# The last segment's output products begin with the linear branch's rows instead of the attention's, and the instruction list is laid out anew

## The chip, the cores and the metric

The kernel runs on one core of one Trainium2 chip. The metric is the device time of one execution in microseconds (us), as the median of several runs. Less is better.

## The reference

Two attention branches read the same input x (2048 rows of 640 columns, bfloat16), and a gate per row mixes their results. Names that begin with A belong to the linear branch, names with B to the memory branch.

```python
# g = sigmoid(sum(x * gate_w));  out = g * A + (1 - g) * B;  32 heads of 20 columns
# A, the linear branch
q, k, v = split(x @ wqkv)
phi(t)  = concat(softmax(t @ w_phi), softmax(-(t @ w_phi)))
A = (phi(q) @ (phi(k).T @ v)) / (phi(q) @ sum(phi(k)) + 1e-6) @ A_wo
# B, the memory branch: 4 segments of 512 rows, one after the other
for s in range(4):
    a_dot = softmax(q_s @ k_s.T * scale + causal mask) @ v_s
    a_mem = (pq @ M) / (pq @ z + 1e-6)        # pq = elu(q_s) + 1
    o_s   = g_h * a_mem + (1 - g_h) * a_dot   # g_h = sigmoid(beta), per head
    M, z  = M + pk.T @ v_s, z + sum(pk)       # pk = elu(k_s) + 1
B = concat(o) @ B_wo
```

Each branch ends in its own product with a 640 x 640 matrix. The kernel puts the gate into the rows of both branches beforehand, so that both products add up in one accumulator.

In the kernel's code the rows of the linear branch are `outA` and `lt.A` with the weight `WoA`, those of the memory branch, which holds the softmax attention, are `oB` and `lt.B` with `WoB`.

## The kernel before

All work is cut into small steps. A step is a function such as `scores` or `tail_mm`, called with a number that says which of its parts to record. The order of all steps of all engines is one string, `ORDER`, of 1609 words, and a loop at the end of the kernel reads it word by word:

```python
for word in "".join(ORDER).split():
    i = done.get(word[:2], 0)
    done[word[:2]] = i + 1
    at = word[2:]
    STEPS[word[0]](WHICH.get(word[:2], int)(i), int(word[1]), int(at) if at.isdigit() else None,
                   sca.copy if at == "a" else vec.tensor_copy)
```

So in a word the letter names the step function, the first digit its part, and what follows is the accumulator bank to use (0 to 3) or an "a" where ScalarE does a copy in place of VectorE. Every engine works through its own instructions strictly in the order of the list. What is queued behind a waiting instruction waits too. The same holds for the DMA queue that SyncE (SP) issues.

Accumulator memory has eight banks. From the fourth score on, four of them are one buffer, `st_ps` (tag `four`), and the other four are single banks, which the digit behind a word names.

The words that matter here:

- `T`, `k`, `K`, `v`, `q`: the first layer. x is turned, and keys, values and queries of the memory branch are projected, evicted, and turned or spread by DMA (`k2`, `q2` on SP's queue). `L0` loads a further 512 rows of x turned (SP), `D0` a turned weight.
- `I`: masks built once on VectorE. `A`, `B`: keys (16 blocks of 128 rows, word `A0` is the product, `A4` the normaliser, words `A3` and `A5` VectorE too) and values (`B0`, `B1` products, `B2`, `B3` evictions, `B4` the gate column) of the linear branch. `S`, `s`, `X`: its sums and its key-value products.
- `P`: scores. `P0` are the products of one score (key times query for four heads, the causal part), `P1` the exponential of all four banks by ScalarE, `P3` the causal masks by GpSimd (one or two instructions). There are 80 scores, five for each two groups of four heads: eight head groups in each of four segments. Each score from the fourth on uses the one four-bank buffer, so `P0` waits for the `P1` before it.
- `U` (segments before the last groups) and `V` (the last four head groups): probabilities times values. In `V`, word `V0` records the products off the diagonal and `V4` those on it, 40 in all for a head group, and `V1` to `V3` divide by the sum on VectorE.
- `Y`, `M`: the query features and the memory of a head group. `M0` are the products, four in the last segment. `M2` to `M4` run on VectorE. `M5` adds memory and attention into the rows `oB` on GpSimd, but the very last on VectorE.
- `f`, `d`, `n`: the linear branch's query features. `f1` and `f2` are exponentials (tile ET), `d` the weights, `n0` and `n1` numerators (six products of a pair of words), `n2` and `n3` on VectorE, `n4` the add into `outA` on GpSimd.
- `l`, `o`: output of the first three segments. `l0` turns the rows of both branches by DMA, `o0` are ten products for half a row block, `o1` evicts, `o2` writes out. `c0` loads a piece of the output weights.
- `G`, `O`: row gates.

The last segment's output is the tail, of four blocks of 128 rows (j = 0 to 3) in two halves of 320 columns, 80 products in all. `t0` (function `tail_A`) turns all linear rows at once into `lt.A`. The three words `b0` (`tail_B`) turn the memory branch's rows into `lt.B`: first columns 0 to 383 (`oB1`), then 384 to 511 (`oB2`), then 512 to 639 (`oB3`), as the head groups finish. The products are in the function `tail_mm`, in four parts: part 0 opens the accumulator of a block, and parts 1, 2 and 3 add to it.

```python
if part == 0 and j in (1, 2):
    if not hasattr(lt, "o2"):
        lt.o2 = banks4("o2_ps")
    t.ps = [lt.o2[:, 2 * j - 2 + h, 0:320] for h in range(2)]
elif part == 0:
    t.ps = getattr(t, "ps", []) + [bank([P, 320], "o_ps", at)]
```

So blocks 1 and 2 use the four-bank buffer of the scores, and their part 0 waits for the last exponential. Blocks 0 and 3 use single banks. Before, part 0 (word `p`, `tail_first`) takes the first three column pieces of `lt.B` (3 products a half), part 1 (word `a`, `tail_mid`) the five pieces of `lt.A` (5 products a half), and parts 2 and 3 (words `e`, `z`) the last two pieces of `lt.B` (1 product a half each). `h` evicts a half and writes the block out.

Of the kernel before, what the change touches and what calls it, by code (L numbers as in the profile page):

```python
# [15 lines left out]
def kernel(  # L16
# [21 lines left out]
    KC = D // P  # L38
# [3 lines left out]
    G = H // 4  # L42
# [48 lines left out]
    a1 = ExitStack()  # L91
# [139 lines left out]
    lt = It()  # L231
# [565 lines left out]
    def tail_mm(j, part, hs, at):  # L797
# [5 lines left out]
        elif part == 0:  # L803
            t.ps = getattr(t, "ps", []) + [bank([P, 320], "o_ps", at)]
        src = (([(lt.B[:, 3 * j + c, :], lt.WoB, c) for c in range(3)]) if part == 0 else
               ([(lt.A[:, KC * j + c, :], lt.WoA, c) for c in range(KC)]) if part == 1 else
# [7 lines left out]
    def tail_first(j, step, at, ev):  # L814
        tail_mm(j, 0, (0, 1) if j in (1, 2) else (step,), at)

    def tail_mid(j, step, at, ev):
        tail_mm(j, 1, (0, 1), at)
# [7 lines left out]
    def tail_out(j, step, at, ev):  # L826
# [5 lines left out]
        else:  # L832
# [8 lines left out]
                 p=tail_first, a=tail_mid, e=tail_next, z=tail_last)  # L841
    WHICH = {**{f"V{j}": lambda i: i + UL for j in range(5)}, "k2": lambda i: 2 * i + 1, "o2": lambda i: 2 * i + 1, "S1": lambda i: 2 * i + 1,
             **{f"M{j}": lambda i: i + G for j in range(2, 6)}, "p1": lambda i: 3 * i}
# [67 lines left out]
    for word in "".join(ORDER).split():  # L911
        i = done.get(word[:2], 0)
# [34 lines left out]
```

## Time and profile before

| | |
|---|---|
| three runs | 287.55, 287.84, 286.81 us |
| median | 287.55 us |
| profiled execution, its own time | 287.34 us |
| its span | 285.6 us |
| TensorE busy | 272.6 us, 3371 instructions |
| ScalarE busy | 239.0 us |
| VectorE busy | 237.2 us |
| GpSimd busy | 183.0 us |
| clock granted to TensorE, mean | 0.998 of full speed |

The profile is of one execution. Its span runs from the first to the last recorded instruction. All work is recorded under one source line, L117, because a small helper keeps every instruction in program order, so rows are told apart by their tiles: `st_ps` are scores, `PT` exponentials and masks, `nd_ps` the products of `V`, `num_ps` numerators, `mem_ps` memory, `o_ps` output products (with `oT` for the first three segments, with `phik` for `lt.A` and `kTs` for `lt.B` in the tail, whose buffers they reuse), `proj` projections, `k_ps` and `v_ps` the linear keys and values, `pf_ps` and `ET` its query features. PE is TensorE, PEld its weight loads, ACT ScalarE, DVE VectorE, POOL GpSimd, and SPq the DMA queue that SyncE issues. A row of the timeline has the start, the length, the engine, the operation, output and inputs and the count, and in brackets the idle time before it and what ended it. In the rows of stretches each engine has its busy time and its count of instructions. The ends of products are modelled, so neighbouring rows may overlap, and the distance from start to start is the surer price.

### The profile page before, as it was taken

What the parts mean: (1) busy time and instruction counts of PE and PEld (TensorE: products, weight loads), DVE (VectorE), ACT (ScalarE), POOL (GpSimd) and SP (SyncE); (2) the same over time, 40 slices, a digit from 0 to 9 for tenths busy, and PEclk for the clock granted to TensorE, in tenths of its full rate; (3) what the DMA queues carried; (4) which work ended last, traced back from release to release, by engine and by line L of the source; (5) the groups of instructions that cost most, each with busy time, mean ns of one, the idle gap of its engine ahead of it and who ended that gap; (6) DMA issues with size and microseconds to landing.
All of it is one profiled execution on the core that took longest, in us unless ns stands there. A gap on an engine that the chain in (4) does not pass through costs nothing.

```text
span 285.6 us, 8511 instructions
## 1 busy us (share of the span) xinstructions
PE 272.6 (95%) x3371; PEld 173.4 (61%) x3393; DVE 237.2 (83%) x577; ACT 239.0 (84%) x259; POOL 183.0 (64%) x305
## 2 busy tenths in 40 slices
PE   7999999999999998999999999999999999999894
PEld 4777676677676545565556566455565556676673
DVE  5969999998889758999778989868999678999922
ACT  2489888897886999998998998999897997988902
POOL 8060000045445856798997799978899898999620
PEclk9999999999999999999999999999999999999999
DMA  7999960100111683356761624183474133564612
GB/s 223 282 239 210 147 149 22 37 2 2 39 21 25 167 116 76 70 108 118 136 97 39 142 63 102 51 128 80 90 83 98 22 92 74 110 118 79 153 38 92
DMA packets 79721, 28.11 MB, mean 98 GB/s; under 512 B 70081, under 2 KB 79681, under 8 KB 79681
## 3 DMA queue, kind: packets, MB, share of 16 engines
q1 hardware_dynamic: 78736, 26.84, 47.1%
q10 hardware_dynamic: 944, 0.74, 0.8%
q8 instruction: 26, 0.43, 0.6%
q14 instruction: 15, 0.11, 0.2%
HBM read 5.61 MB, written 2.62 MB: 29 GB/s over the span
## 4 chain that ended last, share of the span: by engine, by line
PE 67%; ACT 17%; DVE 6%; POOL 5%; issue 2%; DMA 1%; DVEq 0%; ACTq 0%
ACT PT L117 15%; PE proj L117 10%; PE o_ps L117 10%; PE v_ps L117 8%; PE k_ps L117 8%; PE st_ps L117 7%; PE pf_ps L117 5%; PE q_ps L117 5%; PE uv_ps L117 4%; POOL PT L117 2%; PE num_ps L117 2%; PE mem_ps L117 2%; POOL oA L117 2%; DMA WkB<-in_B_wk_dram 1%; PE zb_ps L117 1%
## 5 line engine op out<-in xcount | busy, mean ns | idle before, releaser
L117 ACT ACTIVATE PT<-st_ps 128x2048 bf16<-128x2048 f32 (+1 forms) x83 | 151.0, 1823 | 17.7 <-PE st_ps L117 15.7
L117 POOL TENSOR_SCALAR_AFFINE_SELECT PT<-PT 128x512 bf16<-128x512 bf16 (+2 forms) x116 | 78.9, 694 | 26.5 <-ACT PT L117 26.2
L117 PEld LDWEIGHTS <-xT 128*128 128x128 bf16 x640 | 59.9, 98 | 28.5 <-issue 4.3
L117 PE MATMUL st_ps<-qTp,kTs 32*128 32x384 bf16 (+3 forms) x512 | 31.8, 300 | 5.3 <-ACT PT L117 4.7
L117 ACT ACTIVATE Ek<-k_ps 128x640 bf16<-128x640 f32 x32 | 26.5, 893 | 5.3 <-PE k_ps L117 1.8
L117 POOL TENSOR_TENSOR oA<-t,t 128x320 bf16<-128x320 f32 x32 | 29.2, 914 | 1.3 <-DVE t L117 1.3
L117 DVE TENSOR_TENSOR t<-num_ps,dd 128x320 f32<-128x320 f32 x64 | 28.4, 478 | 0.8 <-PE num_ps L117 0.5
L117 POOL MEMSET qTp<- 128x4096 bf16 x1 | 3.5, 3512 | 39.3 <-ACT vA L117 39.3
L117 PEld LDWEIGHTS <-oT 128*128 128x128 bf16 x240 | 21.9, 98 | 9.8 <-issue 2.2
L117 PEld LDWEIGHTS <-kTs 32*128 32x128 bf16 (+1 forms) x552 | 14.9, 92 | 20.3 <-issue 16.0
L117 PE MATMUL proj<-WkB,xT 128*128 128x320 bf16 x160 | 25.7, 300 | 0.7 <-DVE xT L117 0.4
L117 PE MATMUL proj<-WvB,xT 128*128 128x320 bf16 x160 | 26.1, 300 | 0.0
L117 DVE TENSOR_REDUCE ksum<-Ek 128x64 f32<-128x1280 bf16 x16 | 23.1, 1455 | 2.4 <-ACT Ek L117 2.4
L117 PE MATMUL pf_ps<-xT,WqA 128*128 128x512 bf16 x91 | 24.3, 380 | 0.7 <-DVE uq L117 0.2
L117 PE MATMUL q_ps<-xT,WqB 128*128 128x512 bf16 x87 | 23.7, 380 | 0.9 <-issue 0.3
L117 PE MATMUL v_ps<-WvA,xT 128*128 128x320 bf16 (+1 forms) x160 | 24.2, 300 | 0.0
L117 PE MATMUL k_ps<-qTp,xT 128*128 128x320 bf16 x160 | 23.5, 299 | 0.0
L117 ACT ACTIVATE ET<-pf_ps 128x512 bf16<-128x512 f32 x40 | 21.9, 628 | 0.0
L117 POOL TENSOR_TENSOR oB<-td,tm 128x320 bf16<-128x320 f32 (+4 forms) x25 | 20.5, 824 | 1.2 <-DVE td L117 0.6
L117 DVE CAST uT<-uv_ps 128x512 bf16<-128x512 f32 x28 | 18.8, 670 | 2.4 <-PE uv_ps L117 2.2
L117 PE MATMUL uv_ps<-PT,vB 128*32 128x512 bf16 (+1 forms) x448 | 20.4, 302 | 0.2
L117 PE MATMUL o_ps<-WoA,oT 128*128 128x320 bf16 x120 | 20.3, 300 | 0.0
(114 smaller groups left out, 485.4 us busy)
## 6 DMA issues: line engine op xcount, KB each, us to landing
out_dram<-osb SPq DMA_DIRECT2D x12, 160.0 KB
qTp<-qd SPq DMA_DIRECT2D x8, 128.0 KB
WvB<-in_B_wv_dram SPq DMA_DIRECT2D x1, 800.0 KB
vA<-in_B_wq_dram SPq DMA_DIRECT2D x1, 800.0 KB
WvA<-in_A_wqkv_dram SPq DMA_DIRECT2D x1, 800.0 KB
WoA<-in_A_wo_dram SPq DMA_DIRECT2D x5, 160.0 KB
WoB<-in_B_wo_dram SPq DMA_DIRECT2D x5, 160.0 KB
qTp<-qd SPq DMA_DIRECT2D x8, 96.0 KB
```

Source lines behind the costliest of these rows:

```text
L117: return lambda *a, **k: kept(f(*a, **k))
```

## The change

In `tail_mm`, part 0 and part 1 change their sources: part 0 now opens each block with the five pieces of `lt.A`, and part 1 adds the first three pieces of `lt.B`. The letters follow, so that `a` is still the linear rows (now `tail_first`) and `p` still the memory branch's (now `tail_mid`).

```diff
-        src = (([(lt.B[:, 3 * j + c, :], lt.WoB, c) for c in range(3)]) if part == 0 else
-               ([(lt.A[:, KC * j + c, :], lt.WoA, c) for c in range(KC)]) if part == 1 else
+        src = (([(lt.A[:, KC * j + c, :], lt.WoA, c) for c in range(KC)]) if part == 0 else
+               ([(lt.B[:, 3 * j + c, :], lt.WoB, c) for c in range(3)]) if part == 1 else
                ([(lt.B[:, 4 + 4 * part + j, :], lt.WoB, 1 + part)]))
...
-                 p=tail_first, a=tail_mid, e=tail_next, z=tail_last)
+                 a=tail_first, p=tail_mid, e=tail_next, z=tail_last)
...
-             **{f"M{j}": lambda i: i + G for j in range(2, 6)}, "p1": lambda i: 3 * i}
+             **{f"M{j}": lambda i: i + G for j in range(2, 6)}, "a1": lambda i: 3 * i}
```

`ORDER` is written anew as a whole. It has the same 1609 words but for the renamed ones, one eviction of `B2` that goes from ScalarE to VectorE, and one `o1` and one `U1` that go the other way. From score 33 to score 71 only bank numbers and a few neighbours differ. The words between the last scores, from `P0` of score 71 on, one line for each score:

```diff
 (score 71 and what follows it, to the end)
-P00 U3 P3 n03 U1 P1 n11 o02 U4 n2 U5 n3 n4 o2 n00 n13 o1 U2
-P00 n2 P3 M01 P1 o02 n3 M2 M3 n4 M4 n00 n13 o1 l0 M01 Y0 M5
-P00 n2 o02 P1 Y1 P3 n3 M2 Y2 V00 n4 M3 o1a o2 V4 P3 U3
-P00 M4 M03 P1 o02 V1 U4 M2 U5 V2 M3 M5 o1
-P00 P3 V3 o2 n01 P1 n12 M4 V00 n2 M5 V4 n3 n03 n11 V1 n2 Y0
-P00 V2 n4 n3 b0 o02 P1 Y1 P3 V3 Y2 n4 o1 Y0 Y1
-P00 P3 t0 M03 P1 o01 Y2 M2 M00 M3 o1 Y0 P3
-P00 M4 V02 P1 M2 Y1 M5 V4 M3 o2 p01 Y2 p13 V1 P3 M4
-P00 V2 P1 M00 V3 a0 M2 M5 M3 p00 P3 b0 M4 V02 V4 p01 V1 V2 V3 a0 M5 b0 e0 e0 a0 p00 p12
-z0 z1 e0 h0a h1 z0 z1 a0 h0a h2 h1 h2 z0 z1 e0 h0a h1 z0 z1 h2 h0a h1 h2
+P00 P3 o01 U3 P1 U1 U4 Y2 U5 n02 n13 o2 o1 n2 P3
+P00 U2 n00 n3 P1 n11 M02 n2 o03 n3 n4 M2 M3 n4 M4
+P00 l0 o1 n00 P3 P1 n11 n02 n2 n13 n3 V00 M5 n2 V4 n3 Y0 n4 Y1
+P00 o2 n01 P1 n12 o03 P3 U3 n2 n4 V1 n3 Y2 M01 U4
+P00 V2 o1a n4 M2 o02 P1 M3 P3 t0 M4 V03 o1 U5 Y0 V4 Y1
+P00 P3 V1 M01 Y2 P1 o02 M5 V2 o2 M2 V3 M3 o1a P3
+P00 M4 M00 P1 o02 M2 M3 M5 M01 o1
+P00 P3 M2 b0 V3 a02 P1 M4 a13 M3 M5 V00 M4 Y0 V4 P3 o2 Y1
+P00 V1 P1 Y2 V2 M01 V3 p0 M2 M5 M3 a00 P3 b0 M4 V00 V4 a01 V1 V2 V3 M5 e0 a01 b0 a10 p0 p0
+e0 z0 z1 z0 h0a z1 h1 e0 h0a p0 h1 h2 h2 z0 z1 e0 h0a h1 z0 z1 h2 h0a h1 h2
```

Earlier parts of the list, from score 12 to score 18, and from score 27 to score 33:

```diff
-P00 q00 c0 P1 M6 c0 U3 f03 q2 q1 P3 O0 f1
-P00 f2 c0 v01 f1 M7 k2 K2 k00 f2 U4 v02 P1 v1 P3 k1 M03 f01 v1 U5 M6 q2 K0 K1 M7
-P00 U00 f1 K2 P3 c0 f2 f02 U1 k2 P1 M03 q01 M6 M7 f1 M00 P3 q1 U2
-P00 f2 f03 M6 P1 M7 q2 k01 U00 k1 f1 P3 U3
-P00 U1 f2 k02 U4 U5 P1 U2 v01 k1 d00 v1 k2 K0 K1 P3
-P00 d1 q03 P1 k02 K2 U3 q1a d2 P3
+P00 k1 c0 q02 P1 c0 U3 c0 q03 q1 c0 M7 f1 K2 k2 M01 P3
+P00 f2 q1 f02 P1 M6 U4 q2 f00 P3 f1 M7
+P00 q2 f2 U03 U5 f1 v01 U1 P3 f2 c0 k02 P1 v1 U2 v03 k1 k00 v1 k2 G0 K0 K1 P3
+P00 G1 f01 P1 k1 c0 f02 K2 U3 G2 f1 U4 G3 P3 O0
+P00 f2 U03 U5 f1 k00 U1 f2 v01 P1 U2 k1 M03 M02 v1 d00 M6 k2 M6 M7 K0 K1
+P00 M7 d1 M01 P1 q03 P3 k02 K2 q1a M6 P3
...
-P00 P3 f01 P1 n2 n3 k2 n00 n4 n13 v02 n2 n3 f1 P3 M00 v1 f2
-P00 Y2 M03 P1 U2 n4 f02 M2 M6 M2 M6 M3 M7 M3 c0 U01 M7 M4 f1 q2
...
-P00 f2 P3 k1 U03 U3 Y0 k2 Y1 U4 f00 U1 U5 P1 Y2 M5 U2 q01 M4 f1 P3
+P00 G3 n02 M7 K1 P1 n11 f03 k2 P3 k1 n2 v00 n3 f1 K2 P3
+P00 v1 U2 f2 M02 M01 P1 Y2 v00 n4 M2 q2 f03 M6 M2 M6 M3 M7 v1 Y0 M3 U00 M7 M4 k2 f1 Y1 P3
...
+P00 f2 U4 U1 f02 P3 P1 U2 U5 q00 M5 f1 P3 M4
```

Ahead of score 0 the same products stand in another order. The masks `I0` to `I4` come earlier (in the old list `I0` follows the seventh `k0`, and `I1` to `I4` stand between the ninth and the eleventh `A0`; in the new one all five stand ahead of the first `A0`). The three loads `L0` come earlier, and the key transposes `k2` later.

122 rows, old and new, of the table ORDER are left out of this document.

## The prediction

> **What bounds the kernel now.** I read the page first: shares and chain.
>
> ```profile
> span 285.6 us, 8511 instructions
> ...
> PE 272.6 (95%) x3371; PEld 173.4 (61%) x3393; DVE 237.2 (83%) x577; ACT 239.0 (84%) x259; POOL 183.0 (64%) x305
> ...
> PE 67%; ACT 17%; DVE 6%; POOL 5%; issue 2%; DMA 1%; DVEq 0%; ACTq 0%
> ```
>
> TensorE is the bound: busy 272.6 of 285.6 us, so all its pauses together are 13.0 us, and the change adds and removes no product. Only pauses can move. The profiled execution took 287.34 us, 1.7 us more than its span; the median of the three runs is 287.55. I sum against 287.34 and judge against 287.55, which are 0.07% apart.
>
> The second view is the timeline of TensorE near the end. The list is paced by its 80 scores (word P0; I number them 0 to 79), since each needs the one four-bank buffer that the exponential of the score before it has to leave. Score 71 starts at 249.69, score 79 at 269.52. In brackets stands the pause, and whom it waited for.
>
> ```profile
> 249.69 0.40 PE L117 MATMUL st_ps<-qTp,kTs 32*128 32x384 bf16 x8
> ...
> 254.58 0.40 PE L117 MATMUL st_ps<-qTp,kTs 32*128 32x512 bf16 x4
> 254.91 0.85 PE L117 MATMUL o_ps<-WoA,oT 128*128 128x320 bf16 x5
> 255.60 0.84 PE L117 MATMUL o_ps<-WoB,oT 128*128 128x320 bf16 x5
> 256.27 1.17 PE L117 MATMUL nd_ps<-vB,PT 128*128 128x32 bf16 x40
> 257.38 0.40 PE L117 MATMUL st_ps<-qTp,kTs 32*128 32x384 bf16 x8
> ...
> 259.81 0.40 PE L117 MATMUL st_ps<-qTp,kTs 32*128 32x512 bf16 x4 [0.42 <-ACT PT L117]
> 260.14 0.49 PE L117 MATMUL num_ps<-KV,ET 128*128 128x140 bf16 x6
> 260.58 1.16 PE L117 MATMUL nd_ps<-vB,PT 128*128 128x32 bf16 x40
> ...
> 262.27 0.40 PE L117 MATMUL st_ps<-qTp,kTs 32*128 32x384 bf16 x8 [0.21 <-ACT PT L117]
> ...
> 264.70 0.40 PE L117 MATMUL st_ps<-qTp,kTs 32*128 32x256 bf16 x8 [0.57 <-ACT PT L117]
> 265.03 0.33 PE L117 MATMUL mem_ps<-Mbd,phiq 128*128 128x84 bf16 x4
> 265.19 0.84 PE L117 MATMUL o_ps<-WoA,oT 128*128 128x320 bf16 x5
> ...
> 267.08 0.40 PE L117 MATMUL st_ps<-qTp,kTs 32*128 32x512 bf16 x4 [0.21 <-ACT PT L117]
> ...
> 269.52 0.40 PE L117 MATMUL st_ps<-qTp,kTs 32*128 32x384 bf16 x8
> 269.98 0.31 PE L117 MATMUL mem_ps<-Mbd,phiq 128*128 128x84 bf16 x4
> ...
> 271.95 0.97 PE L117 MATMUL o_ps<-WoB,kTs 128*128 128x320 bf16 x6 [0.30 <-ACT PT L117]
> ```
>
> From start to start, these rows give each kind of work its price: a score 0.33 (254.58 to 254.91), ten output products 1.36 (254.91 to 256.27), the 40 products of one head group's attention 1.11 (256.27 to 257.38), six numerator products 0.44 (260.14 to 260.58), four memory products 0.16 (265.03 to 265.19). They also give the floor. Where less work lies between two scores, TensorE waits for the exponential: 257.38, 259.81, 262.27, 264.70, 267.08, 269.52 are 2.38 to 2.46 apart, mean 2.43. Where more lies there, the work decides: score, ten output products and an attention group are 2.80, and 254.58 to 257.38 is 2.80. So the distance between two scores is the larger of 2.43 and the work that the list puts there. This is the rule of my sum.
>
> **The last eight scores.** Before, scores 71 to 79 take 269.52 − 249.69 = 19.83. I filled the eight distances from the new list. 71–72: ten output products, six numerator products. 72–73: the same and four memory products. 73–74: twelve numerator products, one attention group. 74–75: as 72–73. 75–76: ten output products and an attention group. 76–77: ten output and four memory products. 77–78: ten output, eight memory products. 78–79: the ten products of row block 0's linear rows, and an attention group. With 0.33 for each score, the fourth is 0.33 + 0.44 + 1.36 + 0.16 = 2.29, below the floor, as are the others but two: 75–76 and 78–79 hold 0.33 + 1.36 + 1.11 = 2.80. The new sum is 6 × 2.43 + 2 × 2.80 = 20.18: **0.35 us later** than before. The old list evened this out, with one heavy distance; the new one piles work into two while six wait.
>
> **After the last exponential.** Row blocks 1 and 2 of the tail live in the scores' buffer, so they open only when the last exponential has left it. Before, the wait for it shows 0.30 at 271.95. In the new list six products of row block 0's attention rows fill the time ahead of it, instead of ten of its linear rows; a product is 1.36 / 10 = 0.136, so the wait grows by 4 × 0.136 = 0.54 to 0.84, but it ends with the exponential all the same. Behind it stand, before, 6 output products, an attention group, 58 output products; after, 10, the group, 54. That is 64 in both: nothing. The ten products of row block 1 now cover the masks of the last score (two on GpSimd), which six covered before.
>
> ```profile
> 261.89 2.35 SPq L117 DMA_TRANSPOSE kTs<-oB  x1
> ...
> 264.44 2.50 SPq L117 DMA_TRANSPOSE phik<-oA  x1
> ```
>
> ```profile
> 259.95 1.22 POOL L117 TENSOR_SCALAR_AFFINE_SELECT PT<-PT 128x512 bf16<-128x512 bf16 x2
> 261.14 1.00 POOL L117 TENSOR_TENSOR oB<-td,tm 128x256 bf16<-128x256 f32 x2
> ```
>
> The two transposes change places on SP's queue: linear rows (t0) first, attention rows (b0) past two output DMAs and about two scores later. The first tail product, of linear rows, now stands two scores, over 4.8 us, behind t0's start: 2.50 is covered. b0 waits for GpSimd's add behind mask 76: score 76 starts at 249.69 + 4 × 2.43 + 2.80 = 262.21, its exponential ends some 2.3 later, mask 1.22 and add 1.00 follow, which is 266.8. The attention rows' first use is 0.33 + 0.16 behind score 79's start at 269.87, so 3.6 lie there with 2.35 to cover. If that slack of 1.2 went, the products would slide into the wait for the exponential, of which 0.84 is free. So I cost it at nothing. The last transpose of attention rows (the third b0) still hangs on the last attention group, with 36 output products (4.9 us) between the two in both lists. Evictions and output DMAs close both lists alike.
>
> **The first 33 scores.** Scores 34 to 71 have the same work between them in both lists. Before that, work moves: 1.1 us leaves 13–14 and 1.0 comes into 16–17; 0.3 and 0.7 leave 27–28 and 31–32, 1.0 comes into 28–29. With the floor, the new sum is 0.05 larger up to score 33. Scores 12 to 18 have a second limit, ScalarE, which there also makes the features ET:
>
> ```profile
> 94.31 1.88 ACT L117 ACTIVATE PT<-st_ps 128x2048 bf16<-128x2048 f32 x1 [0.50 <-PE st_ps L117]
> 96.09 2.06 ACT L117 ACTIVATE ET<-pf_ps 128x512 bf16<-128x512 f32 x4
> 97.99 1.93 ACT L117 ACTIVATE PT<-st_ps 128x2048 bf16<-128x2048 f32 x1
> ...
> 108.85 0.73 ACT L117 ACTIVATE ek<-kpads 128x640 bf16<-128x640 bf16 x1
> 109.80 1.88 ACT L117 ACTIVATE PT<-st_ps 128x2048 bf16<-128x2048 f32 x1 [0.22 <-PE st_ps L117]
> ```
>
> From start to start a score's exponential is 1.78 and an ET 0.475. The new list has 2, 4, 0, 4, 0 ET between the exponentials of 12 to 17, which with two ek of 0.73 is 2.73, 3.68, 2.51, 3.68, 2.51: 15.11 (and the exponential of one gate, four elements a row), inside the 15.49 that the old list took from 94.31 to 109.80. So no loss.
>
> Ahead of score 0 the same products stand, in another order:
>
> ```profile
> 0.00:20.00 20.00, 18.28 (x148) 12.73 (x149) 14.74 (x32) 8.87 (x16) 9.97 (x24) 1.00 0.97 249
> ...
> 30.00:40.00 10.00, 10.00 (x83) 7.09 (x82) 10.00 (x17) 8.45 (x18) 0.00 (x0) 1.00 0.84 132
> ```
>
> In these stretches (length, then TensorE, its weight loads, VectorE, ScalarE, GpSimd, clock) TensorE's first 20 us hold its start, and from 30 to 40 it has no pause to gain. VectorE has none there either, so a bank that it empties later can make one; bounds 0 and 1.3 (second rival). The loads of x stand earlier on SP's queue than before, past key transposes that nobody reads until score 0. I take 0.
>
> For waits on evictions and masks in the rearranged places I add 0.2, near the low end of 0 to 1.0 (the larger rival's price below), because the quoted pauses near the end are all ScalarE's. **Sum:** 287.34 + 0.35 + 0.05 + 0.2 = 287.94, so 287.9, its own range 287.4 to 288.5.
>
> **Rivals.** *GpSimd's masks come late (slower).* In 247.9 to 264.4 GpSimd has no air:
>
> ```profile
> 247.90:264.40 16.50, 16.27 (x25) 1.00 0.53 102
> ...
> L117 POOL TENSOR_SCALAR_AFFINE_SELECT PT<-PT 128x1024 bf16<-128x1024 bf16 x15 | 16.6, 1104 | 4.5 <-ACT PT L117 4.5
> ...
> 253.68 0.86 POOL L117 TENSOR_TENSOR oA<-t,t 128x320 bf16<-128x320 f32 x1
> ...
> 256.44 1.03 POOL L117 TENSOR_TENSOR oA<-t,t 128x320 bf16<-128x320 f32 x1
> ```
>
> The new list puts six adds between the masks of scores 71 and 74, and the diagonal products of the second attention group, at the end of 75–76, need mask 74. Walking GpSimd's queue with 0.86 an add: score 71's exponential ends 2.4 after its start, at 252.1, mask 71 (1.22) at 253.3, two adds at 255.0, mask 72 (1.10) at 256.1, two adds at 257.8, mask 73 (half of 1.22) at 258.4, two adds and a small scaling at 260.4, mask 74 (1.22) at 261.6. TensorE starts score 75 at 249.69 + 4 × 2.43 = 259.41 and is through its ten output products and the off-diagonal part (two thirds of 1.11) at 261.8: 0.2 to spare. With 1.03 an add, the mask ends 6 × 0.17 = 1.0 later: TensorE stops 0.8, score 76 and all behind it shift: 287.9 + 0.8 = 288.7. It decides from the point where mask 74 ends after those off-diagonal products. For it: no air. Against: the adds average nearer 0.9 than 1.03. Chance 0.17.
>
> *VectorE holds the banks in the first 60 us (slower).* Ahead of the seventh key block the new list has done one normaliser, one gate column and four small mask copies (words I) more than the old:
>
> ```profile
> L117 DVE RECIPROCAL krec<-ksum 128x64 bf16<-128x64 f32 x16 | 8.4, 537 | 0.0
> ...
> L117 DVE COPY gl<-v_ps 128x1 f32<-128x1 f32 x16 | 2.3, 144 | 0.5 <-ACT vA L117 0.5
> ...
> L117 DVE COPY HZ<-hm 128x40 bf16<-128x40 bf16 x2 | 0.2, 163 | 0.0
> ```
>
> That is 0.54 + 0.14 + 4 × 0.16 = 1.3 of VectorE ahead of the same product. If VectorE is already at TensorE's heels there, 1.3 is lost: 289.2. Against: TensorE has no pause from 30 to 40, and the copies (0.65) move into the first 20 us, where VectorE has 5.26 free. Chance 0.10.
>
> *It comes out faster.* Scores 18 and 27 stand here:
>
> ```profile
> 111.73 0.40 PE L117 MATMUL st_ps<-qTp,kTs 32*128 32x512 bf16 x4
> ...
> 134.26 0.40 PE L117 MATMUL st_ps<-qTp,kTs 32*128 32x256 bf16 x8
> ```
>
> Nine distances in 22.53, where the floor and three slightly heavier ones (2.50) ask 22.1: another order could shed 0.4. The 0.35 shrinks by 0.2 if an attention group costs 1.00 (260.58 to 261.58), and the 0.2 of waits may not come. Together 0.8: 287.1. Chance 0.10.
>
> *The clock falls.* The granted clock is 1.00 in both stretches above and in the GpSimd row's 16.5 us, with pauses of 0.42 and 0.57 among them. If the more frequent pauses halved it, 64 products of 0.136 would cost 8.7 us more: 296.6. Chance 0.01. Beside it: the Trainium skill, "TensorE: Matmul & The Clock Gate", section "A second HAM failure mode: psum-queue depth-cycling", says that frequent short pauses between groups of products can make the clock swing between full and half rate, which speaks against this change. The trace does not show it at these pauses.
>
> **How the numbers follow.** The forecast keeps 0.62. About 0.5%, 1.4 us, is what a measurement can tell from no change: below 286.1 is faster, above 289.0 slower. Slower: half of the VectorE case (0.05), a third of the mask case, where a wait at mask 72 or a later one comes on top (0.06), the clock (0.01), and 0.05 of the forecast's own tail: 0.17. Faster: 0.04, the far end of the faster case. Same: 0.79. The 8-in-10 range reaches from the faster case to both slower ones: 287.0 to 289.2.
>
> **What would show it.** Right: scores 75–76 and 78–79 about 2.8 apart, the other six of the last eight 2.4; a wait of about 0.8 on the last exponential; 64 output products behind it; scores 34 to 71 spaced as before. Wrong: a TensorE wait on GpSimd near score 75, TensorE pauses before score 0 that were not there, score 79 earlier than score 71 + 19.8, or a clock below 1.00.

## The result, and the profile after

| | before | after |
|---|---|---|
| median | 287.28 us | 288.08 us |
| lowest and highest | 286.81 to 287.84 | 287.78 to 288.83 |
| runs | 12 | 12 |
| profiled execution: time, span | 287.34, 285.6 us | 288.82, 287.1 us |

The changed kernel takes 1.0030 of the time of before, 95% interval 1.0022 to 1.0039: 0.86 us slower, with 0.63 to 1.12 inside the interval. That is less than the 0.5% that was called no change. The forecast was 287.9, range 287.0 to 289.2.

The page of after, shares and chain:

```profile
span 287.1 us, 8521 instructions
...
PE 274.1 (95%) x3371; PEld 173.7 (60%) x3393; DVE 237.3 (83%) x576; ACT 239.3 (83%) x260; POOL 185.0 (64%) x305
...
PE 63%; ACT 24%; POOL 4%; issue 4%; DVE 3%; DMA 2%; DVEq 0%; ACTq 0%; POOLq 0%; SPq 0%
```

The chain has moved from TensorE (67% before) towards ScalarE (17% before, now 24%). That is no measure of the loss: 7% of the span are 20 us, and the kernel lost 0.86. The waits of TensorE's scores that the profile puts down to the exponential even fell, from 4.7 to 4.4 us in sum. What changed is read from the timeline of TensorE near the end of after. The rows are the scores 71, 75, 76, 78 and 79, and then everything behind the last exponential:

```profile
250.48 0.40 PE L117 MATMUL st_ps<-qTp,kTs 32*128 32x384 bf16 x8
...
260.18 0.40 PE L117 MATMUL st_ps<-qTp,kTs 32*128 32x512 bf16 x4
...
262.97 0.40 PE L117 MATMUL st_ps<-qTp,kTs 32*128 32x384 bf16 x8
...
267.79 0.40 PE L117 MATMUL st_ps<-qTp,kTs 32*128 32x512 bf16 x4 [0.21 <-ACT PT L117]
...
270.59 0.40 PE L117 MATMUL st_ps<-qTp,kTs 32*128 32x384 bf16 x8
271.36 0.32 PE L117 MATMUL mem_ps<-Mbd,phiq 128*128 128x84 bf16 x4 [0.38 <-DVE phiq L117]
271.52 0.98 PE L117 MATMUL o_ps<-WoB,kTs 128*128 128x320 bf16 x6
273.02 1.52 PE L117 MATMUL o_ps<-WoA,phik 128*128 128x320 bf16 x10 [0.53 <-ACT PT L117]
274.38 1.16 PE L117 MATMUL nd_ps<-vB,PT 128*128 128x32 bf16 x40
275.39 1.52 PE L117 MATMUL o_ps<-WoA,phik 128*128 128x320 bf16 x10
276.74 0.43 PE L117 MATMUL o_ps<-WoB,kTs 128*128 128x320 bf16 x2
277.01 1.52 PE L117 MATMUL o_ps<-WoA,phik 128*128 128x320 bf16 x10
278.37 3.69 PE L117 MATMUL o_ps<-WoB,kTs 128*128 128x320 bf16 x26
282.29 0.97 PE L117 MATMUL o_ps<-WoB,kTs 128*128 128x320 bf16 x6 [0.22 <-DVE vB L117]
```

Scores 75 and 76 are 2.79 apart, 78 and 79 are 2.80, and 71 to 79 take 270.59 − 250.48 = 20.11 (19.83 before). The last row is new. The 26 products ahead of it are through at 278.37 + 26 × 0.136 = 281.91, and the six start at 282.29: a pause of 0.38 where before had none. The same moment on the engines that evict (ScalarE, VectorE):

```profile
280.61 0.43 ACT L117 CAST vB<-o_ps 128x320 bf16<-128x320 f32 x1 [7.64 <-PE o_ps L117]
280.75 0.49 DVE L117 CAST vB<-o_ps 128x320 bf16<-128x320 f32 x1 [3.65 <-PE o_ps L117]
281.29 0.43 ACT L117 CAST vB<-o_ps 128x320 bf16<-128x320 f32 x1 [0.25 <-PE o_ps L117]
...
281.75 0.49 DVE L117 CAST vB<-o_ps 128x320 bf16<-128x320 f32 x1 [0.51 <-ACT vB L117]
```

The first two are the halves of row block 0, which lie in two single banks: they run side by side. The other two are row block 1, whose halves lie in the scores' four-bank buffer together with row block 2. They run one after the other, and the first of the six, which writes row block 2's part of that buffer, starts when the second has ended (281.75 + 0.49 = 282.24). To the waits the buffer is one thing, though the halves touch different banks. Before, the same place looks like this (the ten products follow row block 1's last product, the six begin with row block 2's):

```profile
279.48 1.52 PE L117 MATMUL o_ps<-WoA,phik 128*128 128x320 bf16 x10
...
279.68 0.42 ACT L117 CAST vB<-o_ps 128x320 bf16<-128x320 f32 x1 [0.25 <-PE o_ps L117]
...
280.83 0.98 PE L117 MATMUL o_ps<-WoB,kTs 128*128 128x320 bf16 x6
```

Between row block 1's last product and row block 2's next the old list has ten products (1.36), the new one eight (1.09). But two of the eight, row block 2's word `e0`, write the same buffer and stand ahead of row block 1's evictions in the list. They are the 19th and 20th of the 26, so they are through at 278.37 + 20 × 0.136 = 281.09, and the eviction starts 0.20 behind them, at 281.29. Before, it starts 0.20 behind row block 1's last product (279.48, 279.68). From the eviction's start to the next product in the buffer 1.00 passes (281.29 to 282.29). So 1.20 has to be covered: ten products do it, and the six that are left in after, 0.82, leave the 0.38 open. That `e0` holds the eviction is read from these starts; no run moves it alone.

For the rest of the time I read the start of every score in both profiles, and in those of the experiments. Three marks are enough: score 0, score 70, and the end of the span.

| profile | list up to 70 | from 70 on | score 0 at | 0 to 70 | 70 to the end |
|---|---|---|---|---|---|
| before | old | old | 62.66 | 184.57 | 38.37 |
| after | new | new | 63.31 | 184.72 | 39.07 |
| e1 | old | new | 63.27 | 184.31 | (seam) |
| e2 | new | old | 63.31 | 184.69 | (seam) |
| e3 | new | new, edited | 62.57 | 184.62 | 38.71 |
| e4 | new | new, edited | 63.61 | 184.71 | 38.68 |
| e5 | old | new | 62.92 | 184.39 | 39.09 |
| e6 | new | old | 63.35 | 184.71 | 38.44 |
| e7 | old | old, sources exchanged | 63.24 | 184.32 | 39.34 |
| e8 | old | new, edited | 63.16 | 184.31 | 38.63 |
| e9 | old | old, evened | 63.31 | 184.33 | 38.66 |
| e10 | old | new, edited | 62.75 | 184.36 | 38.19 |

From score 0 to 70 the old list takes 184.31 to 184.39 in six profiles and 184.57 in the one shown with the prediction, which has a distance of 2.68 between scores 58 and 59 where five of the six have 2.43 or 2.44 (e5 2.56). The new list takes 184.62 to 184.72. The new layout costs about 0.35 there, the new tail about 0.7. Score 0 itself starts anywhere from 62.57 to 63.61 with either list; the 0.65 between the two profiled executions is scatter.

### The profile page after: what moved, and what is told of

It is laid out like the page before. It is cut to its first block, busy times and chain, and to the rows that moved or that the text cites. A ratio compares the mean times of both kernels' runs of the same rounds, so it can differ in the third digit from the quotient of the medians.

```text
span 287.1 us, 8521 instructions
## 1 busy us (share of the span) xinstructions
PE 274.1 (95%) x3371; PEld 173.7 (60%) x3393; DVE 237.3 (83%) x576; ACT 239.3 (83%) x260; POOL 185.0 (64%) x305
## 4 chain that ended last, share of the span: by engine, by line
PE 63%; ACT 24%; POOL 4%; issue 4%; DVE 3%; DMA 2%; DVEq 0%; ACTq 0%; POOLq 0%; SPq 0%
ACT PT L117 19%; PE proj L117 10%; PE v_ps L117 8%; PE k_ps L117 8%; PE o_ps L117 7%; PE st_ps L117 7%; PE pf_ps L117 5%; PE q_ps L117 5%; PE uv_ps L117 3%; ACT eq L117 2%; POOL oA L117 2%; PE mem_ps L117 1%; PE zb_ps L117 1%; PE num_ps L117 1%; ACT ET L117 1%
## 5 line engine op out<-in xcount | busy, mean ns | idle before, releaser
L117 POOL TENSOR_SCALAR_AFFINE_SELECT PT<-PT 128x512 bf16<-128x512 bf16 (+2 forms) x116 | 80.4, 707 | 24.6 <-ACT PT L117 24.1
L117 PE MATMUL proj<-WkB,xT 128*128 128x320 bf16 x160 | 26.8, 305 | 0.2 <-DVE xT L117 0.2
L117 DVE CAST uT<-uv_ps 128x512 bf16<-128x512 f32 x27 | 18.2, 674 | 5.4 <-PE uv_ps L117 5.0
```

The source lines that it names most:

```text
L117: return lambda *a, **k: kept(f(*a, **k))
```

## The experiments

Each kernel was timed in five rounds against the kernel before. The ratios in the expectations are to the kernel before; "the theory" is that the loss sits in the tail and in scores 24 to 26.

**e1: the new tail on the old list.**

```diff
 (the list of before up to score 70, its words from there replaced; tail_mm as in after)
-P00 U2 Y1 o02 P1 P3 n2 n3 ... (before, to the end)
+P00 U2 Y1 o03 P1 P3 n2 n3 ... (after, to the end)
```

> The list of before up to score 70, and behind it the list of after with its tail_mm. Theory (the loss lies in the tail): the profile of after lost 0.28 between scores 71 and 79 and 0.38 behind the last exponential (a wait on the evictions of row block 1), so this kernel is 0.66 slower than before: about 287.9, ratio 1.0023. Scores 75-76 and 78-79 are 2.8 apart, and the last six output products start with a pause on an eviction. Rival (the newly laid front and middle carry the loss): no difference from before, 287.3, ratio 1.000.

Measured: 289.11 against 287.58, ratio 1.0053 (1.0035 to 1.0071). More than the whole change, so it fits neither. The timeline behind score 70:

```profile
248.86 0.84 PE L117 MATMUL o_ps<-WoA,oT 128*128 128x320 bf16 x5 [0.88 <-DVE t L117]
```

The output products of this score now use bank 3 where the old list has bank 2, and bank 3 still waits for VectorE to evict a numerator. Score 71 comes 3.39 behind score 70 instead of 2.45. The seam made a wait of its own. This run tells nothing of the change.

**e2: the old tail on the new list.**

```diff
 (the list of after up to score 70, its words from there replaced; tail_mm as in before)
-P00 U2 Y1 o03 P1 P3 n2 n3 ... (after, to the end)
+P00 U2 Y1 o02 P1 P3 n2 n3 ... (before, to the end)
```

> The list of after up to score 70, and behind it the list of before with its tail_mm. Theory: +0.48 in scores 24 to 26, where VectorE has no air, -0.34 in single distances of scores 43 to 59 and in the first 24, so +0.14 in all: about 287.4, ratio 1.0005. Rival (the loss is in the front and the middle): +0.7 or so, 288.0, ratio 1.0024. The 0.65 that score 0 came late in the profile of after: by the theory it is scatter of one execution and not there in the median; if it belongs to the list, this profile shows score 0 at 63.3 again, and the time is 0.65 more.

Measured: 289.16 against 287.58, ratio 1.0053 (1.0036 to 1.0070), with score 71 coming 3.80 behind score 70: the same seam. From score 0 to 70 it takes 184.69, as after does. Score 0 stands at 63.31, which the expectation named as the sign that the late start belongs to the list; e3, with the same opening, has it at 62.57, so it does not.

**e3: more products between row block 1's end and row block 2's.**

```diff
-... b0 a10 p0 p0 e0 z0 z1 z0 h0a z1 h1 e0 h0a p0 h1 h2 h2 z0 ...
+... b0 p0 p0 e0 z0 z1 z0 h0a z1 h1 e0 h0a a10 p0 h1 h2 h2 z0 ...
```

> After, with the second half of row block 3's linear products (five) moved from ahead of row block 1's and 2's attention products to just behind row block 1's last product. Theory: the 0.38 that the first last product of row block 2 waited for the evictions of row block 1 is covered by 5 x 0.136 = 0.68 of products and goes: 0.38 faster than after, about 287.7 against 288.1, ratio to before 1.001. Rival (those evictions only look like the cause; the end is set by the evictions and the write behind the last product): no difference from after, ratio 1.0028. Second rival: 31 products instead of 36 now stand between the last attention group and row block 0's last product, which needs the last transpose; if that was tight, a pause of up to 0.5 appears there.

Measured: 288.08 against 287.58, ratio 1.0019 (1.0008 to 1.0030). The timeline of TensorE:

```profile
276.86 2.88 PE L117 MATMUL o_ps<-WoB,kTs 128*128 128x320 bf16 x20
...
279.58 0.84 PE L117 MATMUL o_ps<-WoA,phik 128*128 128x320 bf16 x5
...
280.26 1.79 PE L117 MATMUL o_ps<-WoB,kTs 128*128 128x320 bf16 x12
```

No row has a bracket: the pause is gone, and no pause on the last transpose has come. Eleven products (1.50) now stand behind `e0`, more than the 1.20 that the evictions need. From score 70 to the end it takes 38.71 against 39.07, 0.36 less, as expected. The times alone (1.0019 and 1.0030) would not tell the two apart; the rows do.

**e4: half of row block 0's products behind score 79.**

```diff
-P00 P3 M2 b0 V3 a02 P1 M4 a13 M3 M5 V00 M4 Y0 V4 P3 o2 Y1
-P00 V1 P1 ...
+P00 P3 M2 b0 V3 a02 P1 M4 M3 M5 V00 M4 Y0 V4 P3 o2 Y1
+P00 a13 V1 P1 ...
```

> After, with the second half of row block 0's linear products (five) moved from between scores 78 and 79 to behind score 79. Theory (the larger of the floor of 2.43 and the work sets each distance): 78-79 falls from 2.80 to the floor, as its work falls to 0.33 + 0.68 + 1.11 = 2.12; the five go into the wait for the last exponential; 0.37 faster than after, about 287.7, ratio to before 1.0015. Rival (the last exponential is not set by score 79's start but by ScalarE or by the masks): 78-79 shorter, the wait shorter by no more than the five products bring, the end where it was, ratio 1.0028.

Measured: 288.13 against 287.58, ratio 1.0014 (1.0003 to 1.0024). The timeline, score 79 and the first product behind the last exponential:

```profile
270.53 0.40 PE L117 MATMUL st_ps<-qTp,kTs 32*128 32x384 bf16 x8
...
272.96 1.52 PE L117 MATMUL o_ps<-WoA,phik 128*128 128x320 bf16 x10 [0.18 <-ACT PT L117]
```

78 to 79 falls from 2.80 to 2.46, and 272.96 − 270.53 = 2.43 is what it was in after (273.02 − 270.59). So the last exponential does hang on score 79's start, and the whole 0.34 comes through. The rival falls.

**e5 and e6: the seams mended.** As e1 and e2, with the banks behind the seam renamed as the list ahead of it has them:

```diff
 (e5: in all words of the new tail)
-bank 1, 2, 3
+bank 3, 1, 2
 (e6: in all words of the old tail)
-bank 1, 2, 3
+bank 2, 3, 1
```

> As e1 (the list of before up to score 70, behind it the list and the tail_mm of after), but with the banks renamed behind the seam (2 to 1, 3 to 2, 1 to 3) as the list of before has them, so that no product at the seam meets a bank that is not yet evicted. Theory (e1's extra loss was the seam: score 71 came 3.39 behind score 70 instead of 2.45): that goes, 70-71 is 2.45 again, and what is left is the tail's own cost, 0.28 + 0.38 = 0.66 against before, ratio 1.0023, about 288.2 beside a before of 287.58. Rival (the tail of after costs more or less than its profile showed): another ratio, 1.000 if the front carries the loss.

> As e2 (the list of after up to score 70, behind it the list and the tail_mm of before), with the banks renamed behind the seam the other way (1 to 2, 2 to 3, 3 to 1). Theory: 70-71 is 2.45 again instead of 3.80, and what is left is the front's and the middle's own cost, 0.48 - 0.34 = 0.14 against before, ratio 1.0005. Rival: the new front costs more, up to the whole 0.8, ratio 1.0028.

Measured: e5 288.08 against 287.43, ratio 1.0020 (1.0007 to 1.0032); e6 288.01 against 287.43, ratio 1.0012 (1.0000 to 1.0024). In both, score 71 is 2.46 behind score 70 again. e5 has after's distances in the tail: 71 to 79 in 269.87 − 249.77 = 20.10, and the same pause:

```profile
249.77 0.40 PE L117 MATMUL st_ps<-qTp,kTs 32*128 32x384 bf16 x8
...
269.87 0.40 PE L117 MATMUL st_ps<-qTp,kTs 32*128 32x384 bf16 x8
...
281.58 0.97 PE L117 MATMUL o_ps<-WoB,kTs 128*128 128x320 bf16 x6 [0.22 <-DVE vB L117]
```

So by these marks about two thirds of the loss is the tail and one third the front; the two ratios alone leave more room (0.20 to 0.92 us and 0.00 to 0.69 us). For the front I had expected 0.14; the table has 0.35. The profile of before had flattered it: its 0.25 between scores 58 and 59, which I had counted as a gain of the new list, is not there in most runs of the old one.

**e7: the exchange alone.** The old list word for word, only the sources and the letters exchanged:

```diff
 (tail_mm and the letters as in after)
-... M3 o2 p01 Y2 p13 V1 P3 M4 P00 V2 P1 M00 V3 a0 M2 ...
+... M3 o2 a01 Y2 a13 V1 P3 M4 P00 V2 P1 M00 V3 p0 M2 ...
```

> The list of before word for word, with only the two sources exchanged (and the letters p and a, so that part 0 stays part 0): linear rows first, without a new layout. Theory: ten products instead of six stand between scores 78 and 79, 0.33 + 1.11 + 1.36 = 2.80 against the floor of 2.43, +0.37; at the end only row block 3's six products instead of ten stand between row block 1's last product and row block 2's, 0.82 instead of 1.36 of cover, so the wait for row block 1's evictions shows with about 0.5 to 0.65. Together +0.9 against before, ratio 1.003. Rival (the exchange is free where the list stays, and the new layout alone is what costs): ratio 1.000.

Measured: 288.68 against 287.43, ratio 1.0038 (1.0023 to 1.0052). From score 70 to the end it takes 39.34, 0.97 more than before, where 0.9 was expected. The sizes are not quite the expected ones:

```profile
267.41 0.40 PE L117 MATMUL st_ps<-qTp,kTs 32*128 32x512 bf16 x4 [0.21 <-ACT PT L117]
...
270.40 0.40 PE L117 MATMUL st_ps<-qTp,kTs 32*128 32x384 bf16 x8
...
280.08 1.79 PE L117 MATMUL o_ps<-WoB,kTs 128*128 128x320 bf16 x12
...
282.10 0.97 PE L117 MATMUL o_ps<-WoB,kTs 128*128 128x320 bf16 x6 [0.22 <-DVE vB L117]
```

78 to 79 is 2.99, 0.19 above the work of 2.80: the attention group takes 1.20, as it does in before at the same place (267.41 to 268.61), and the ten products take 1.46; why is not shown. The pause at the end is 282.10 − (280.08 + 12 × 0.136) = 0.39, and here no `e0` but six products alone stand behind row block 1's last one: 1.20 − 0.82 = 0.38. The exchange costs by itself; the new tail got back some of it (39.07 against 39.34), and the new front lost 0.35.

**e8: fill the waits.** The new tail on the old list (as e5), with the edits of e3 and e4, and five products of row block 3 ahead of row block 1's:

```diff
-"a1": lambda i: 3 * i}
+"a1": lambda i: 3 * i, "a0": lambda i: (0, 3, 1, 2)[i]}
...
-P00 V1 P1 Y2 V2 M03 V3 p0 M2 M5 M3 a00 P3 b0 M4 V00 V4 a03 V1 V2 V3 ...
+P00 a12 V1 P1 Y2 V2 M03 V3 p0 M2 M5 M3 a00 a0 P3 b0 M4 V03 V4 a0 V1 V2 V3 ...
```

> The list of before up to score 70, behind it the tail of after with the banks as in e5 and three edits: the second half of row block 0's linear products behind score 79 (as e4), the second half of row block 3's behind row block 1's last product (as e3), and the first half of row block 3's ahead of the last exponential's end, where TensorE still waits. Theory: +0.66 of the tail of after, -0.36 and -0.36 for the first two (as e3 and e4 measured in their profiles), and -0.33 for the third (0.33 of pause is left in e4 ahead of row block 1's first product, five products are 0.68): -0.39 against before, ratio 0.9986. Rival: the third edit only moves the pause, because the masks or the last transposes then end last: ratio 0.9998.

Measured: 287.73 against 287.43, ratio 1.0010 (1.0000 to 1.0020). It went as the rival says, the pause moved, but the kernel is slower than the rival's 0.9998. The tail takes 38.63, and a row shows what ends last now:

```profile
276.18 2.34 PE L117 MATMUL o_ps<-WoB,kTs 128*128 128x320 bf16 x16
...
278.93 0.99 PE L117 MATMUL o_ps<-WoB,kTs 128*128 128x320 bf16 x6 [0.41 <-DMA kTs<-oB]
```

With 26 products between the last attention group and row block 0's last ones, the last transpose is late. The bracket says 0.41; reckoned from the starts, as the 0.38 above, the pause is 278.93 − (276.18 + 16 × 0.136) = 0.57. With that the tail adds up: the 39.09 of e5, less 0.36, 0.36 and 0.33, and 0.57 more, is 38.61. In e3, with 31 products, no such pause shows.

**e9: even out the old list.**

```diff
-            t.all = bpt.tile([P, 4, 512], BF16, name="PT")
+            t.all = (halves[0].pool.tile([P, 4 * D], BF16, name="oB")[:, 0:2048].rearrange(
+                "p (b n) -> p b n", b=4) if n == 74 else bpt.tile([P, 4, 512], BF16, name="PT"))
...
-... V00 n4 M3 o1a o2 V4 P3 U3 P00 M4 M03 P1 o02 V1 ...
+... V00 n4 M3 o1a o2 P3 U3 P00 V4 M4 M03 P1 o02 V1 ...
```

> The kernel before with its one heavy distance evened: the 16 diagonal products of head group 28 go from between scores 73 and 74 to behind score 74, and the probabilities of score 74 get a buffer of their own (the rows oB of the other segments, which nobody reads any more), so that its exponential need not wait for those products. Theory (the larger of floor and work): 73-74 falls from 2.80 to about 2.43, 74-75 stays at the floor with 0.33 + 0.44 + 0.16 + 1.36 = 2.29, and all behind it comes 0.37 earlier: ratio 0.9987. Rival: the division and the add of head group 28, one score later, meet a full VectorE, and the pause only moves to scores 74 to 76: ratio 1.000.

Measured: 287.69 against 287.67, ratio 1.0005 (0.9994 to 1.0017). 73 to 74 falls to 2.45 as expected, but 74 to 75 grows to 2.95, for a reason that neither theory had:

```profile
258.46 1.88 ACT L117 ACTIVATE oB<-st_ps 128x2048 bf16<-128x2048 f32 x1 [0.76 <-DMA oT<-oB]
```

The exponential of score 74 waited for the last output transpose of the other segments, which reads the buffer lent to it. The gain was there and my loan ate it. An evened old list without such a wait was not run.

**e10: e8 with both ends mended.** The same loan for score 76, two scores later; and the five products back ahead of the transpose's first use, with two of row block 3 (its word `e0`) in their place:

```diff
 (the buffer of e9 for n == 76)
-... V02 o1 U5 Y0 V4 Y1 P00 P3 V1 ...
+... V02 o1 U5 Y0 Y1 P00 V4 P3 V1 ...
...
-... e0 b0 p0 p0 e0 z0 z1 z0 h0a z1 h1 e0 h0a a13 p0 h1 h2 h2 z0 z1 e0 h0a h1 z0 z1 ...
+... e0 b0 a13 p0 p0 e0 z0 z1 z0 h0a z1 h1 e0 h0a p0 h1 e0 h2 h2 z0 z1 h0a h1 z0 z1 ...
```

> e8 with two more edits. The 16 diagonal products of head group 29 go from between scores 75 and 76 to behind score 76, whose probabilities get a buffer of their own (the rows oB of the other segments). And the second half of row block 3's linear products goes back ahead of row block 0's last products, which in e8 waited 0.41 for the last transpose; in its place the two products of e of row block 3 stand behind row block 1's last ones. Theory: 75-76 falls from 2.80 to 2.43 (-0.37), the pause on the transpose goes (-0.41), ten products (1.36) instead of thirteen now cover the about 1.47 that row block 1's evictions take, so that up to 0.1 of pause shows there and the end comes 0.03 earlier in sum; together -0.40 against e8, ratio 0.9996 to before. Rival: mask 74, which in e8 ended 0.24 ahead of the diagonal products, or VectorE behind them sets score 76 or 77 instead: ratio 1.001 as e8.

Measured: 287.10 against 287.67, ratio 0.9985 (0.9973 to 0.9996), where 0.9996 was expected. The scores 75 and 76, and the last row of products:

```profile
259.27 0.40 PE L117 MATMUL st_ps<-qTp,kTs 32*128 32x512 bf16 x4
...
261.72 0.40 PE L117 MATMUL st_ps<-qTp,kTs 32*128 32x384 bf16 x8
...
276.62 4.62 PE L117 MATMUL o_ps<-WoB,kTs 128*128 128x320 bf16 x32
```

75 to 76 is 2.45, and the tail takes 38.19 against 38.63 in e8 (−0.44, expected −0.40). The split distance is what brought it: 71 to 79 falls from 19.75 to 19.33, while score 79 to the end stays (16.42 and 16.40). The pause of 0.57 on the transpose is gone, but three others came. The memory products behind score 79 wait some 0.26 longer for phiq (VectorE's uq ahead of it takes 0.68 beside a GpSimd mask, 0.28 in e8). The 32 products take 4.62 where the 26 of after take 3.69, 0.93 for 0.82 of work: with eight products behind `e0`, 1.20 − 1.09 = 0.11 is open. And the span runs on about 0.2 longer behind the last product. This version is a little faster than before (by 0.11 to 0.78 us): linear rows first is not slow as such, if the heavy distances are split. Whether the old order with the same loan would be faster still was not run.

**e11: GpSimd's add behind the mask.** Scores 24 to 26 take 5.65 in after (127.31 to 132.96) and 5.17 in before. Two of VectorE's copies between its own memories take longer there, uk and uq: 0.58 each in after, 0.43 and 0.32 in before. This run moves one GpSimd word of after:

```diff
-... k03 q1 n4 Y0 P00 Y1 P3 ...
+... k03 q1 Y0 P00 Y1 P3 n4 ...
```

> After, with one word moved on GpSimd's queue: the add of the numerators that stood ahead of the mask of score 25 goes behind it. Theory (what scores 24 to 26 lost in the new list is VectorE's copies between its own memories that take longer beside a GpSimd add): uq, 0.58 in after beside that add and 0.32 in before beside a mask, falls to about 0.32, and 25-26 from 2.98 to about 2.72; 0.26 faster than after, ratio 1.0021. Rival (VectorE is late there because the list gives it more work, or the add when it comes later slows another of its instructions): 25-26 or 26-27 keep the time, ratio 1.003.

Measured: 288.70 against 287.67, ratio 1.0035 (1.0023 to 1.0047); 25 to 26 is 3.07 instead of 2.98. The theory fell. The rows of both engines in before, in after and in e11:

```profile
127.39 0.43 DVE L117 TENSOR_SCALAR uk<-kpads 128x640 bf16<-128x640 bf16 x1
...
129.07 1.27 POOL L117 TENSOR_SCALAR_AFFINE_SELECT PT<-PT 128x512 bf16<-128x512 bf16 x2
...
129.52 0.32 DVE L117 TENSOR_SCALAR uq<-qTp 128x512 bf16<-128x512 bf16 x1
```

```profile
127.97 0.58 DVE L117 TENSOR_SCALAR uk<-kpads 128x640 bf16<-128x640 bf16 x1
...
130.03 0.86 POOL L117 TENSOR_TENSOR oA<-t,t 128x320 bf16<-128x320 f32 x1 [0.98 <-DVE t L117]
...
130.47 0.58 DVE L117 TENSOR_SCALAR uq<-qTp 128x512 bf16<-128x512 bf16 x1
```

```profile
129.56 1.22 POOL L117 TENSOR_SCALAR_AFFINE_SELECT PT<-PT 128x512 bf16<-128x512 bf16 x2 [0.73 <-ACT PT L117]
...
130.26 0.67 DVE L117 TENSOR_SCALAR uq<-qTp 128x512 bf16<-128x512 bf16 x1
```

In before the first of the two masks ends at 129.07 + 0.635 = 129.71, and uq at 129.84. In after the add ends at 130.89, uq at 131.05. In e11 the second mask ends at 130.78, uq at 130.93. So uq ends about 0.15 behind the GpSimd instruction that ran when it started, mask or add. In these rows only how much of that instruction is left counts.

**e12: uq where GpSimd idles.**

```diff
-... l0 U1 P1 n12 q01 n2 P3 n3 k03 q1 n4 Y0 P00 Y1 P3 ...
+... l0 U1 P1 Y0 Y1 n12 q01 n2 P3 n3 k03 q1 n4 P00 P3 ...
```

> After, with uq (VectorE) and its eq (ScalarE) of one head group moved up by one score, from behind score 25 to behind the exponential of score 24, ahead of two numerator evictions. The rows of e11 say against its theory that it is not the kind of GpSimd instruction that counts: uq ended 0.14 to 0.17 behind the end of the GpSimd instruction that ran when it started, be it mask or add. Theory (uq can't run while a GpSimd instruction runs): at its new place, about 129.1 in the profile of after, GpSimd idles between a mask (ended 129.05) and an add (from 130.03), so uq takes 0.23 as it does elsewhere without a GpSimd instruction, instead of 0.58; VectorE gains 0.35, and of the 5.65 between scores 24 and 26 (5.17 in before) 0.2 to 0.35 go; about 0.3 faster than after, ratio 1.002. Rival (uq's length goes with its data or its neighbours on VectorE; VectorE only has too much to do): uq stays near 0.58 and 24 to 26 at 5.65; ratio 1.003.

Measured: 288.43 against 287.44, ratio 1.0029 (1.0018 to 1.0041). VectorE's row, with the mask that ends just ahead of it:

```profile
128.50 0.72 POOL L117 TENSOR_SCALAR_AFFINE_SELECT PT<-PT 128x512 bf16<-128x512 bf16 x1
...
129.24 0.28 DVE L117 TENSOR_SCALAR uq<-qTp 128x512 bf16<-128x512 bf16 x1
```

uq takes 0.28, and 25 to 26 falls from 2.98 to 2.68, the 0.3 expected. It is now below the 2.73 of before although uk still takes 0.58 (at 128.14), so uk is not needed to explain this distance. 24 to 25 stays at 2.66, against 2.44 in before. TensorE's rows in after, from score 24 to score 25:

```profile
127.31 0.40 PE L117 MATMUL st_ps<-qTp,kTs 32*128 32x384 bf16 x8
127.64 0.49 PE L117 MATMUL num_ps<-KV,ET 128*128 128x140 bf16 x6
128.10 1.24 PE L117 MATMUL q_ps<-xT,WqB 128*128 128x512 bf16 x4
129.21 0.84 PE L117 MATMUL proj<-WkB,xT 128*128 128x320 bf16 x5
129.98 0.39 PE L117 MATMUL st_ps<-qTp,kTs 32*128 32x512 bf16 x4
```

No row shows a wait: the new list puts six numerator products here that the old one has behind score 26, and the distance is above the floor. 26 to 27 falls from 2.51 to 2.43 for it. Products of the same kinds and number took 2.51 there and take 2.67 here; the 0.16 between the two stays open.

But 28 to 29 grows from 3.46 to 3.57, and in sum 0.26 less stands between scores 0 and 70 (184.46 against 184.72), which the time itself doesn't show (1.0029 against 1.0030, both uncertain by 0.001). The mechanism is shown at its place; its worth for the whole is not.

## Why the prediction was right, step by step

The time came out 0.18 above the forecast and inside its own range. As a difference, 0.60 was forecast and 0.86 measured (0.63 to 1.12); the times look closer than that because the median of before is 0.06 below the 287.34 of the sum. Two of the steps were mis-sized, both too low, and one of them was a wait that the prediction denied.

- **The last eight scores, 0.35.** Right: 20.11 against the predicted 20.18 and 19.83 before, so +0.28. 75 to 76 and 78 to 79 are the two heavy distances. e4 took one away and got 0.34, e10 the other.
- **After the last exponential, nothing.** This is the step that failed. Equal numbers of products stand behind it, and the wait ahead of it is about as predicted (0.38 on phiq and 0.53 on the exponential, 0.91 in sum against 0.84). But the sentence "Evictions and output DMAs close both lists alike" was false: evictions of row block 1 hold row block 2's last products. They need 1.20, for which the old list had ten products of cover (1.36) and the new one six (0.82). It costs 0.38, e3 took it away, and e7 shows that it comes with the exchange itself.
- **The first 33 scores and the waits on evictions, 0.05 and 0.2.** The front costs about 0.35 (e6, and the table). Scores 12 to 17 are as predicted, 15.48 in both lists, with no loss on ScalarE; 28 to 29 is 3.46, balanced by its neighbours. The loss sits at 24 to 26, +0.48, and other distances give a little back. It has two parts. 25 to 26, +0.25, is a wait on VectorE, longer by uq's wait for GpSimd; e12 shows it at its place. 24 to 25, +0.23, shows no wait on VectorE: six numerator products moved in, a move that the prediction's list does not name; it is worth 0.08, which 26 to 27 gives back, and the rest stays open. So the 0.2 for waits came near in size, but it hung on no row, and that is luck.
- **Ahead of score 0, nothing.** Right, and it is exact. TensorE's second projection starts at 6.77 in before, and score 0 55.89 behind it; in after it starts at 7.42, and score 0 again 55.89 behind it (55.89 or 55.90 in every profile of the table). All the scatter of score 0 is there in the first 8 us. So is most of the 1.5 us by which TensorE's busy time on the page grew with the same number of products: it is busy 6.28 of the first 8.00 us in before, and 7.36 of the first 8.65 in after, where the first projection's five products take 1.54 instead of 0.84. The rows of the second projection:

```profile
6.77 0.85 PE L117 MATMUL proj<-WkB,xT 128*128 128x320 bf16 x5 [0.42 <-DVE xT L117]
```

```profile
7.42 0.85 PE L117 MATMUL proj<-WkB,xT 128*128 128x320 bf16 x5 [0.20 <-DVE xT L117]
```

- **The rivals.** VectorE in the first 60 us falls by the same rows. GpSimd's masks near score 75: no row of TensorE waits there in after, so it did not happen; the spare 0.2 was real, since in e8 mask 74 ends at 261.79 and its products start at about 262.0. The faster case fell, since the waits came: the nine distances from score 18 to 27 take 22.94 in after, not less than the 22.53 of before. The clock: the granted clock of after was 0.999 in the profiled execution, so the swing named beside that rival did not show. The sign "a clock below 1.00" was too strict, since before itself has 0.998: it is 1.00 from score 70 to 282.0 and 0.81 behind that, where TensorE has nothing left to do.

In sum 0.28 and 0.38 in the tail and 0.35 in the front make 1.0, against 0.86 (0.63 to 1.12) measured.

## What to carry to other kernels

Where one buffer's release sets a floor for each step, count the work between two steps: products moved into a step cost what goes beyond the floor (here 0.37 of ten products' 1.36), and splitting the heavy step gives it back. When products at the very end change places, look at what evicts the accumulators behind them: here the tiles that share one buffer were evicted one after the other and held each other's next products, and the cover counts from the last product that the eviction itself has to wait for. When two lists are spliced, the banks at the seam must be the same, and an experiment whose own edit makes a wait tells nothing until that wait is named.

## What the runs showed of the hardware

VectorE's `uq`, bf16 from SBUF to SBUF, does not run beside a GpSimd instruction in these rows, it waits. In the profile of after 21 rows of a single uq start while a GpSimd instruction runs; 20 of them end 0.14 to 0.17 behind its end, whether they take 0.28 or 1.01, and the one that doesn't starts where the second of two masks follows the first. The three that meet no GpSimd instruction take 0.23 to 0.28. The Trainium skill, "SBUF — State Buffer", section "Who interferes with whom", says that VectorE in a two-port mode and GpSimd hold a shared port pair as an exclusive lock for a whole instruction, and that the order of issue decides who blocks. The rows of this case agree, down to the remainder of the running instruction as the price; which mode uq runs in, no row shows.

The opening of one and the same list scatters by 1.0 us, from 62.57 (e3) to 63.61 (e4) at score 0, and from there to score 70 the profiles of one list agree within 0.1 but for before's. A profile of a single execution is better compared from a mark inside it than from its start.
